# A deep cross network on one core: tail operand kept in two lane orders, 512-column row tiles, corner among the row tiles, new head and tail order

## The chip, the cores and the metric

The kernel runs on 1 core of one Trainium2 chip. The metric is the time of one execution on the device in microseconds (us). Before the change it is 141.67 us, the median of 3 runs.

Engines, by the names of the profile: PE is TensorE (matmuls; PEld are its weight loads), DVE is VectorE, ACT is ScalarE, POOL is GpSimd, SP is SyncE, which here only issues DMAs. PE reads SBUF and writes PSUM, here 8 banks of 512 fp32 columns on 128 partitions (the tensor `ps`); DVE and ACT read it from there.

## The reference

```python
B, F, D, L = 4096, 26, 16, 6
Din = min(F * D, 1024)

def reference(x0, ws, bs):
    x = x0
    for l in range(ws.shape[0]):
        x = x0 * (x @ ws[l] + bs[l]) + x
    return x
```

`x0` is 4096 x 416, `ws` six matrices of 416 x 416, `bs` six rows of 416, all bf16. Since x is x0 times some factor at every layer, x = x0 * s, the kernel keeps the sum of all `x @ ws[l]` so far in PSUM and never clears it between layers: after layer l, x = x0 * (1 + sums + biases up to l). That is one DVE instruction per tile, (PSUM + bias) * x0, where the bias column holds 1 plus the sum of the biases.

## The kernel before

**Tiles.** The 4096 rows of x are worked in four stages (`s`) of 1024. Everything is held transposed: features on partitions, rows of x on columns. The 416 features are three chunks of 128 (`m` for outputs, `k` for inputs) and a tail of 32. Each of the three chunks has two halves of 512 rows (`half`), which fill PSUM banks 0 to 2 and 3 to 5. The tail's 1024 rows are folded: group `g` of 256 rows lies on the partitions 32g to 32g + 31 (a lane) of one tile with 256 columns, in bank 6. Bank 7 (`SPARE`) is for transposes.

**One layer on PE** (the loop over `l` in L212 to L299), in program order:

1. `main(0)`: for each of three output chunks and three input chunks four matmuls of 32 output columns each, which lie side by side in the array (column tiles, `tile_mm`), each 128 x 32 weights against 512 columns: 36 matmuls, half 0.
2. Row tiles (L264 to L280): the tail as input, 32 partitions deep, for all three chunks and both halves: 12 matmuls of 256 columns. Lane g sits in the row group 32g of the array. The tail group g belongs to half g // 2 and to columns (g % 2) * 256 of that half's banks, so lanes 0 and 1 write into the same banks, and lanes 2 and 3. [...]
3. The tail as output: 12 column tiles of 256 columns from the three chunks, and 4 more with the corner of the matrix (tail to tail) from `wc_sb`, a block-diagonal copy of the corner that POOL makes with eight copies (`corner`, L144).
4. `main(1)`: half 1, 36 column tiles.

**Around it.** DVE takes each of the six banks of a layer with one instruction of 128 x 512 (L348) and writes `xT_sb` (or `xo_sb` in the last layer). It waits for `s_ti` (row tiles done) for half 0 and for `s_mb` for each chunk of half 1. PE's next `main(0)` waits for half 0 (`s_xa`), its next row tiles for half 1 (`s_xb`) and for the tail (`s_xt`). The tail goes from bank 6 by ACT (L387, adds the bias) to `t32_sb`, and POOL (L158) multiplies it by x0's tail (`x0t_sb`) into `xt_sb`. x0's tail is brought in by small PE transposes (`tail_transposes`) and an ACT copy (`tail_in`), for stage 0 between `main(0)` and the row tiles of the first layer, for the others in layers 1 to 3 of stage 0.

**Start.** SP issues the two halves of `xin_sb` (the first 512 rows), a piece of the tail, a DMA transpose of rows 512 to 1023 and then weights; ACT issues the weights of layer 0, the biases and the tail's weights of layer 0. PE runs 20 dummy matmuls of 128 columns (`NFILL`) and then transposes `xin_sb` chunk by chunk as the two halves land; DVE and ACT copy the results to `x0T_sb`.

**End.** The first three stages leave by DMA transposes. The last stage is transposed by PE (L312) after DVE's last instructions, ACT and DVE copy the results to `o_sb`, and SP issues four stores of 208 KB.

Of the kernel before, what the change touches and what calls it, by code (L numbers as in the profile page):

```python
# [11 lines left out]
def bass_standalone__dcn_v2_cross__recsys_kernel(  # L12
# [8 lines left out]
    NC = 3  # L21
# [9 lines left out]
    TAIL, SPARE = 6, 7  # L31
    NFILL = 20

    with ExitStack() as es:
# [6 lines left out]
        wt_sb = sb("wt_sb", [128, L, D])  # L41
        wc_sb = sb("wc_sb", [128, L, 128])
# [3 lines left out]
        x0t_sb = sb("x0t_sb", [128, NS, G])  # L46
        xT_sb = sb("xT_sb", [128, 2, NC, SB])
        xt_sb = sb("xt_sb", [128, 2, G])
        t32_sb = sb("t32_sb", [128, 2, G], FP32)
        xo_sb = sb("xo_sb", [128, NS, NC, SB])  # L50
# [4 lines left out]
        ones_sb = sb("ones_sb", [128, 128])  # L55
# [17 lines left out]
        s_tp, s_te = sem("s_tp"), sem("s_te")  # L73
        s_row, s_ti, s_to, s_mb = sem("s_row"), sem("s_ti"), sem("s_to"), sem("s_mb")
        s_xa, s_xb = sem("s_xa"), sem("s_xb")
        s_ta, s_xt = sem("s_ta"), sem("s_xt")
        s_oT, s_ot, s_otc = sem("s_oT"), sem("s_ot"), sem("s_otc")
        s_pT, s_out = sem("s_pT"), sem("s_out")
        s_oet, s_oe = sem("s_oet"), [sem("s_oe%d" % i) for i in range(4)]
# [6 lines left out]

        @block.sync
        def _(sp):
            for h in range(2):
                sp.dma_start(xin_sb[:, 2 * h:2 * h + 2, :], x0_v[:, 2 * h:2 * h + 2, :]).then_inc(s_xin[h], 16)  # L90
            sp.dma_start(xtl_sb[:, 4:JS, :], x0_v[:, 4:JS, DF:D]).then_inc(s_xtl0, 16)
            sp.dma_start_transpose(x0T_sb[:, :, H:SB], x0[H:SB, 0:DF]).then_inc(s_x0T[0], 16)
            for l in range(1, L):
                sp.dma_start(w_sb[:, l, :, :], wmain(l)).then_inc(s_w[l], 16)
                if l == 1:
                    for g in range(4):
                        sp.dma_start(
                            wt_sb[32 * g:32 * g + 32, 1:L, :], ws[1:L, DF:D, :].rearrange("l p n -> p l n")
                        ).then_inc(s_wt[1], 16)
# [20 lines left out]
            for i in range(4):  # L120
                j = (NS - 1) * JS + 2 * i
                if i == 0:
                    sp.wait_ge(s_oet, 1)
                sp.wait_ge(s_oe[i], 1)
                sp.dma_start(out_v[:, j:j + 2, :], o_sb[:, j:j + 2, :]).then_inc(s_out, 16)
            sp.wait_ge(s_out, 16 * (NS + 3))

        @block.gpsimd
        def _(pool):
            pool.memset(ones_sb[:, :], 1.0).then_inc(s_ones, 1)  # L130
            pool.memset(bsa_sb[0:1, :], 1.0).then_inc(s_set, 1)
            pool.wait_ge(s_ones, 1)
            pool.affine_select(
                out=ident[:, :], in_=ones_sb[:, :], pattern=[[-1, 128]],
                compare_op=ALU.is_equal, fill=0.0, base=0, channel_multiplier=1,
            ).then_inc(s_set, 1)
            pool.affine_select(
# [4 lines left out]
            pool.wait_ge(s_set, 4)  # L142

            def corner(i, a, b):  # L144
                pool.wait_ge(s_wt[i], 64)
                for g in range(4):
                    p = slice(32 * g, 32 * g + 32)
                    pool.tensor_copy(out=wc_sb[p, a:b, p], in_=wt_sb[p, a:b, DF:D]).then_inc(s_wc, 1)  # L148
                    pool.wait_ge(s_wc, 4 * i + g + 1)

            corner(0, 0, 1)
            for s in range(NS):
                pool.wait_ge(s_te, s + 1)
                for l in range(L):
                    n = s * L + l + 1
                    pool.wait_ge(s_ta, n)
                    dst = xot_sb[:, s, :] if l == L - 1 else xt_sb[:, (l + 1) % 2, :]
                    pool.tensor_tensor(  # L158
                        out=dst, in0=t32_sb[:, n % 2, :], in1=x0t_sb[:, s, :], op=ALU.mult
                    ).then_inc(s_xt, 1)  # L160
                    if n == 1:
                        pool.wait_ge(s_xt, 1)
                        corner(1, 1, L)
# [8 lines left out]
        def _(pe):  # L172
            def tile_mm(dst, lhsT, rhs, q, start, stop):
                return pe.matmul(  # L174
                    dst, lhsT=lhsT, rhs=rhs, start=start, stop=stop,
                    skip_group_check=True, tile_position=(0, 32 * q),
                )

            def tail_transposes(s):
                for r in range(2):  # L180
                    for g in range(4):
                        j = 2 * g + r
                        src = xin_sb[:, j, DF:D] if s == 0 and j < 4 else xtl_sb[:, s * JS + j, :]
                        ins = tile_mm(
                            ps[32 * g:32 * g + 32, SPARE, r * 128:(r + 1) * 128],
                            src, ident[:, :], g, True, True,
                        )
                ins.then_inc(s_tp, 1)

            pe.wait_ge(s_ones, 1)  # L190
            for i in range(NFILL):
                pe.matmul(ps[:, SPARE, 0:128], lhsT=ones_sb[:, :], rhs=ones_sb[:, :], start=True, stop=True)  # L192
            pe.wait_ge(s_set, 4)
            for h in range(2):
                pe.wait_ge(s_xin[h], 16)
                for c in range(NC):
                    for j in range(2 * h, 2 * h + 2):
                        ins = pe.transpose(  # L198
                            out=psT[:, NC * (1 - h) + c, (j % 2) * 128:(j % 2 + 1) * 128],
                            in_=xin_sb[:, j, c * 128:(c + 1) * 128], identity=ident[:, :],  # L200
                        )
                    ins.then_inc(s_inT, 1)
            pe.wait_ge(s_bs, 16)
            for c in range(NC):
                for q in range(4):
                    f0 = c * 128 + 32 * q
                    ins = tile_mm(ps[32 * q:32 * q + 32, SPARE, c * 8:c * 8 + L], bsa_sb[:, f0:f0 + 32], u_sb[:, :], q, True, True)
            for q in range(4):
                ins = tile_mm(ps[32 * q:32 * q + 32, SPARE, NC * 8:NC * 8 + L], bsa_sb[:, DF:D], u_sb[:, :], q, True, True)
            ins.then_inc(s_cbp, 1)  # L210

            for s in range(NS):  # L212
                for l in range(L):
                    n = s * L + l
                    if l == 0:
# [6 lines left out]
                    def main(half, waits):  # L222
                        o = off + half * H
                        for m in range(NC):
                            for k in range(NC):
                                if waits and m == 0:
                                    waits(k)
                                for q in range(4):
                                    f0 = m * 128 + 32 * q
                                    ins = tile_mm(  # L230
                                        ps[32 * q:32 * q + 32, NC * half + m, :],
                                        w_sb[:, l, k, f0:f0 + 32], src[:, k, o:o + H], q,
                                        l == 0 and k == 0 and half == 0, True,
                                    )
                            if half == 1:
                                ins.then_inc(s_mb, 1)

                    def wait_a(k):
                        if n > 0:
                            pe.wait_ge(s_xa, NC * (n - 1) + k + 1)  # L240
                        if n == 0:
                            pe.wait_ge((s_inD, s_inA, s_inD)[k], (3, 2, 4)[k])
                        elif l == 0 and k == 0:
                            pe.wait_ge(s_x0T[s], 16)
# [3 lines left out]
                    main(0, wait_a)  # L248

                    if n == 0:  # L250
                        pe.wait_ge(s_xtl0, 16)
                        pe.wait_ge(s_cb, 1)
                        tail_transposes(0)
                    if s == 0 and l < 2:
                        pe.wait_ge(s_wt[l], 64)
                        pe.wait_ge(s_wc, 4 * (l + 1))
                    if n == 0:
                        pe.wait_ge(s_te, 1)
                    else:
                        pe.wait_ge(s_xt, n)  # L260
                        pe.wait_ge(s_xb, NC * n)
# [173 lines left out]
```

## Time and profile before

| | |
|---|---|
| median of 3 runs | 141.67 us (141.16, 141.67, 142.47) |
| the profiled execution's own time | 141.47 us |
| its span, first to last instruction | 138.9 us |
| granted TensorE clock, mean | 0.989 |
| PE busy | 131.3 us, 2506 matmuls |
| DVE busy | 98.7 us, 149 instructions |
| ACT, POOL busy | 17.7 us, 21.1 us |
| HBM read, written | 3.22 MB, 3.41 MB |

The times of single instructions and waits are from the profiled execution. A line such as `57.20 0.76 PE L272 MATMUL ps<-xt_sb,wt_sb 32*128 32x256 bf16 x12` of the timeline means: from 57.20 us after the start of the span, for 0.76 us, twelve matmuls of line 272, weights 32 deep and 128 wide, against 256 columns. Such a matmul's duration holds its way through the array; the next may begin long before it ends, so the pace is read from starts. What stands in brackets is the idle time of the engine before the line, and what ended it. In the chain of work a line is a start, a length and what it was.

### The profile page before, as it was taken

The numbers are of one execution on the slowest core, as the hardware profiler recorded it, in microseconds if no ns is written. First come the engines' busy times: TensorE is split into PE (matmuls) and PEld (weight loads), VectorE is DVE, ScalarE is ACT, GpSimd is POOL, SyncE is SP. The second block draws the span as 40 slices with busy tenths as digits, with TensorE's granted clock in tenths as the row PEclk, the third lists the DMA queues.
The fourth block names the chain that finished last, engine by engine and source line by source line (L and its number), as shares of the span: only waits on it lengthen the run. The fifth ranks groups of instructions, "written<-read, shape, count | busy, mean of one in ns | idle before, by whom it ended". The sixth has DMA issues, their size and how long they took to land.

```text
span 138.9 us, 5386 instructions
## 1 busy us (share of the span) xinstructions
PE 131.3 (94%) x2506; PEld 67.2 (48%) x2506; DVE 98.7 (71%) x149; ACT 17.7 (13%) x36; POOL 21.1 (15%) x44
## 2 busy tenths in 40 slices
PE   6799999999999999999999999999999999999950
PEld 5435445545445545545445445545545445444440
DVE  0306797696697697688688679679669669669660
ACT  0601011121001001101101101101101101101170
POOL 5022211011011021011011021101101201101100
PEclk9999999999999999999999999999999999999995
DMA  4999799910008933000009652000009960000007
GB/s 118 267 245 329 99 218 233 195 33 0 5 0 76 176 126 129 0 5 0 5 0 118 133 168 82 5 0 5 5 0 186 65 221 29 5 0 7 0 1 244
DMA packets 32946, 12.26 MB, mean 88 GB/s; under 512 B 25239, under 2 KB 32925, under 8 KB 32925
## 3 DMA queue, kind: packets, MB, share of 16 engines
q1 hardware_dynamic: 32320, 11.50, 41.3%
q10 hardware_dynamic: 604, 0.43, 1.1%
q8 instruction: 19, 0.31, 1.0%
q14 instruction: 3, 0.02, 0.0%
HBM read 3.22 MB, written 3.41 MB: 48 GB/s over the span
## 4 chain that ended last, share of the span: by engine, by line
PE 90%; DVE 3%; DMA 3%; ACT 1%; SPq 0%; issue 0%
PE ps L174 77%; PE ps L272 12%; DVE xo_sb L348 3%; DMA xin_sb<-in_x_dram 3%; PE ps L312 1%; PE ps L198 1%; ACT o_sb L403 1%; SPq L90 0%; ACT x0t_sb L377 0%
## 5 line engine op out<-in xcount | busy, mean ns | idle before, releaser
L348 DVE SCALAR_TENSOR_TENSOR xT_sb<-ps,cb_sb,x0T_sb 128x512 bf16<-128x512 f32 x120 | 80.9, 743 | 26.1 <-PE ps L272 26.1
L174 PE MATMUL ps<-xT_sb,w_sb 128*32 128x512 bf16 (+1 forms) x1680 | 91.1, 364 | 0.0
L174 PEld LDWEIGHTS ps<-xT_sb,w_sb 128*32 128x32 bf16 x1680 | 42.9, 97 | 37.2
L158 POOL TENSOR_TENSOR xt_sb<-t_sb,x0t_sb 128x256 bf16<-128x256 f32 x20 | 13.5, 674 | 86.3 <-ACT t_sb L387 86.3
L387 ACT ACTIVATE t_sb<-ps,cb_sb 128x256 f32<-128x256 f32 x24 | 11.4, 474 | 103.0 <-PE ps L174 103.0
L174 PE MATMUL ps<-x0T_sb,w_sb 128*32 128x512 bf16 (+1 forms) x336 | 20.4, 389 | 0.0
L348 DVE SCALAR_TENSOR_TENSOR xo_sb<-ps,cb_sb,x0T_sb 128x512 bf16<-128x512 f32 x24 | 16.2, 744 | 4.3 <-PE ps L272 4.3
L272 PE MATMUL ps<-xt_sb,wt_sb 32*128 32x256 bf16 x240 | 15.2, 274 | 0.0
L174 PEld LDWEIGHTS ps<-x0T_sb,w_sb 128*32 128x32 bf16 x336 | 9.0, 101 | 8.4 <-issue 1.6
L272 PEld LDWEIGHTS ps<-xt_sb,wt_sb 32*128 32x128 bf16 x240 | 6.0, 91 | 13.5 <-issue 8.5
L174 PE MATMUL ps<-xt_sb,wc_sb 128*32 128x256 bf16 x80 | 5.7, 273 | 0.0
L158 POOL TENSOR_TENSOR xot_sb<-t_sb,x0t_sb 128x256 bf16<-128x256 f32 x4 | 2.7, 674 | 17.8 <-ACT t_sb L387 17.8
L330 DVE COPY x0T_sb<-ps 128x256 bf16<-128x256 bf16 x4 | 1.2, 292 | 5.2 <-PE ps L198 5.0
L272 PE MATMUL ps<-x0t_sb,wt_sb 32*128 32x256 bf16 x48 | 3.0, 274 | 0.6 <-ACT x0t_sb L377 0.6
L192 PE MATMUL ps<-ones_sb 128*128 128x128 bf16 x20 | 2.3, 313 | 1.1 <-POOL ones_sb L130 1.1
L148 POOL COPY wc_sb<-wt_sb 32x32 bf16<-32x32 bf16 (+1 forms) x8 | 2.1, 258 | 5.7 <-DMA wt_sb<-in_ws_dram 5.3
L272 PEld LDWEIGHTS ps<-x0t_sb,wt_sb 32*128 32x128 bf16 x48 | 1.2, 91 | 3.0 <-issue 2.0
L198 PE MATMUL ps<-ident,xin_sb 128*128 128x128 bf16 x12 | 1.6, 305 | 1.1 <-DMA xin_sb<-in_x_dram 1.1
L377 ACT ACTIVATE x0t_sb<-ps 128x256 bf16<-128x256 f32 x4 | 1.5, 383 | 8.4 <-PE ps L174 8.4
L403 ACT ACTIVATE o_sb<-ps 128x768 bf16<-128x768 bf16 x3 | 2.3, 809 | 2.2 <-PE ps L312 2.2
L192 PEld LDWEIGHTS ps<-ones_sb 128*128 128x128 bf16 x20 | 2.0, 147 | 1.1 <-POOL ones_sb L130 1.1
L312 PE MATMUL ps<-ident,xo_sb 128*128 128x128 bf16 x24 | 1.7, 220 | 0.8 <-DVE xo_sb L348 0.8
(28 smaller groups left out, 16.2 us busy)
## 6 DMA issues: line engine op xcount, KB each, us to landing
out_dram<-o_sb SPq DMA_DIRECT2D x3, 832.0 KB, 4.2
w_sb<-in_ws_dram SPq DMA_DIRECT2D x5, 312.0 KB, 4.9
out_dram<-o_sb SPq DMA_DIRECT2D x4, 208.0 KB, 2.4
wt_sb<-in_ws_dram SPq DMA_DIRECT2D x4, 130.0 KB, 3.9
xin_sb<-in_x_dram SPq DMA_DIRECT2D x2, 208.0 KB, 3.5
w_sb<-in_ws_dram ACTq DMA_DIRECT2D x1, 312.0 KB, 3.8
xtl_sb<-in_x_dram SPq DMA_DIRECT2D x1, 192.0 KB, 7.3
o_sb<-xo_sb SPq DMA_TRANSPOSE x9, 4.4
```

The source lines that it names most:

```text
L148: pool.tensor_copy(out=wc_sb[p, a:b, p], in_=wt_sb[p, a:b, DF:D]).then_inc(s_wc, 1)
L158: pool.tensor_tensor(out=dst, in0=t32_sb[:, n % 2, :], in1=x0t_sb[:, s, :], op=ALU.mult).then_inc(s_xt, 1)
L174: return pe.matmul(dst, lhsT=lhsT, rhs=rhs, start=start, stop=stop, skip_group_check=True, tile_position=(0, 32 * q),)
L192: pe.matmul(ps[:, SPARE, 0:128], lhsT=ones_sb[:, :], rhs=ones_sb[:, :], start=True, stop=True)
L198: ins = pe.transpose(out=psT[:, NC * (1 - h) + c, (j % 2) * 128:(j % 2 + 1) * 128], in_=xin_sb[:, j, c * 128:(c + 1) * 128], identity=iden ...
L272: ins = pe.matmul(ps[:, NC * (g // 2) + m, (g % 2) * G:(g % 2) * G + G], lhsT=wt_sb[p, l, m * 128:(m + 1) * 128], rhs=srct[p, :], start=l ...
L312: ins = pe.transpose(out=psT[:, banks[i], jj * DF + c * 128:jj * DF + (c + 1) * 128], in_=xo_sb[:, s, c, j * 128:(j + 1) * 128], identity= ...
L330: dve.tensor_copy(out=x0T_sb[:, c, h * 256:(h + 1) * 256], in_=psT[:, NC * (1 - h) + c, 0:256]).then_inc(s_inD, 1)
L348: dve.scalar_tensor_tensor(out=dst, in0=ps[:, NC * half + c, :], scalar=cb_sb[:, c, l:l + 1], in1=x0T_sb[:, c, o:o + H], op0=ALU.add, op1= ...
L377: act.activation(out=x0t_sb[:, s, :], in_=ps[:, SPARE, 0:G], func=ACTF.Copy).then_inc(s_te, 1)
L387: act.activation(out=t32_sb[:, n % 2, :], in_=ps[:, TAIL, 0:G], func=ACTF.Identity, bias=cb_sb[:, NC, l:l + 1],).then_inc(s_ta, 1)
L403: act.activation(out=o_sb[:, j0 + 2 * i:j0 + 2 * i + 2, 0:DF], in_=psT[:, (SPARE, 0, 3, 4)[i], 0:2 * DF].rearrange("p (j d) -> p j d", d=D ...
```

## The change

The change has five parts.

**The tail in two lane orders.** `xt_sb` and `x0t_sb` become twice as wide. The left half is what it was; in the right half lanes 0 and 1 have changed places, and lanes 2 and 3. ACT makes the right half with four copies of 32 partitions (`swap_lanes`) after POOL's product; for x0's tail of stage 0 PE makes a second set of transposes and DVE copies it, for the later stages ACT does it in layer 2. In lanes 0 and 2 the two halves together are 512 columns: the whole of a half of a stage, in order.

**Row tiles.** A row tile of lane 0 (or 2) is now 512 columns and fills a whole bank. In `part` 0 lane 0 does bank 0 and lane 1 bank 2, as two matmuls of 256 columns; lanes 2 and 3 do the same with banks 3 and 5. In `part` 1 lane 0 does bank 1 and lane 2 bank 4; lanes 1 and 3 do the corner, into banks 6 and 7. So no two lanes share a bank at any time, and `s_row` and its waits are gone. `wt_sb` holds, per lane, only the columns that the lane needs, and `wc_sb` (with 32 zero columns more) is filled by two POOL DMAs; the eight copies are gone.

**The tail as output** lies in two banks (6 for lanes 0 and 1, 7 for 2 and 3), and ACT evicts it in two halves of 64 partitions. Its four column tiles for the corner are gone. The spare halves of banks 6 and 7 take the transposes of x0's tail, one stage per stage, in layer 1.

```diff
-                    for i, jobs in enumerate((
-                        ((0, 0), (1, 1), (2, 0), (3, 1)), ((0, 2), (2, 2)),
-                        ((0, 1), (1, 0), (2, 1), (3, 0)), ((1, 2), (3, 2)),
-                    )):
-                        if i >= 2:
-                            pe.wait_ge(s_row, 3 * n + i - 1)
-                        for g, m in jobs:
...
+                    def row(g, dst, lhsT, cols, start):
+                        return pe.matmul(
+                            dst, lhsT=lhsT, rhs=srct[lane(g), cols], start=l == 0 and start, stop=True,
+                            skip_group_check=True, tile_position=(32 * g, 0),
+                        )
+
+                    lo, hi = slice(0, G), slice(G, 2 * G)
+                    for part in range(2):
+                        for h in range(2):
+                            g, wm = 2 * h, slice(part * 128, part * 128 + 128)
+                            row(g, ps[:, NC * h + part, :], wt_sb[lane(g), l, wm], slice(0, H), h == 1)
+                            g += 1
+                            if part == 0:
+                                row(g, ps[:, NC * h + 2, hi], wt_sb[lane(g), l, 0:128], lo, h == 1)
+                            else:
+                                row(g, ps[:, 6 + h, lo], wc_sb[lane(g), l, 0:128], lo, True)
+                        for h in range(2):
+                            g = 2 * h + 1
+                            if part == 0:
+                                ins = row(g, ps[:, NC * h + 2, lo], wt_sb[lane(g), l, 0:128], hi, False)
+                            else:
+                                ins = row(g, ps[:, 6 + h, lo], wc_sb[lane(g), l, 32:160], hi, False)
                     ins.then_inc(s_ti, 1)
...
+            def swap_lanes(buf, done):
+                for g in range(4):
+                    ins = act.activation(out=buf[lane(g), G:2 * G], in_=buf[lane(g ^ 1), 0:G], func=ACTF.Copy)
+                ins.then_inc(done, 1)
...
+                    if l < L - 1:
+                        act.wait_ge(s_xt, n)
+                        swap_lanes(xt_sb[:, (l + 1) % 2, :], s_sw)
```

PE's order in a layer, before. In these rows `xT_sb` and `w_sb` are the chunks and their weights, `xt_sb`, `wt_sb` and `wc_sb` the tail, its weights and its corner; 32x512 is a column tile, 128x256 a row tile.

```order
L174 MATMUL ps<-xT_sb,w_sb 32x512 x36
L272 MATMUL ps<-xt_sb,wt_sb 128x256 x12
L174 MATMUL ps<-xT_sb,w_sb 32x256 x12
L174 MATMUL ps<-xt_sb,wc_sb 32x256 x4
L174 MATMUL ps<-xT_sb,w_sb 32x512 x36
```

PE's order in a layer, after.

```order
L312 MATMUL ps<-xt_sb,wt_sb 128x512
L312 MATMUL ps<-xt_sb,wt_sb 128x256
L312 MATMUL ps<-xt_sb,wt_sb 128x512
L312 MATMUL ps<-xt_sb,wt_sb 128x256 x3
L312 MATMUL ps<-xt_sb,wt_sb 128x512
L312 MATMUL ps<-xt_sb,wc_sb 128x256
L312 MATMUL ps<-xt_sb,wt_sb 128x512
L312 MATMUL ps<-xt_sb,wc_sb 128x256 x3
L195 MATMUL ps<-xT_sb,w_sb 32x256 x12
L195 MATMUL ps<-xT_sb,w_sb 32x512 x72
```

The corner stands among the row tiles, and the tail's column tiles are followed by the chunks at once. ACT's order after, from the first layer of stage 0 on; before, each layer had the single eviction `t_sb` of 128x256, and the copies to `x0t_sb` in layers 1 to 3.

```order
L468 ACTIVATE t_sb<-ps,cb_sb 64x256 x2
L450 ACTIVATE xt_sb<-xt_sb 32x256 x4
L468 ACTIVATE t_sb<-ps,cb_sb 64x256 x2
L476 ACTIVATE x0t_sb<-ps 64x256 x2
L450 ACTIVATE xt_sb<-xt_sb 32x256 x4
L468 ACTIVATE t_sb<-ps,cb_sb 64x256 x2
L450 ACTIVATE xt_sb<-xt_sb 32x256 x4
L450 ACTIVATE x0t_sb<-x0t_sb 32x256 x4
```

A layer has six ACT instructions where it had one, and four of them stand between POOL's product and PE's next row tiles.

**Head.** The dummy matmuls are 13 of 256 columns, and 3 more between the two halves of the transposes. The second half of `xin_sb` is issued by ACT, layer 0's weights by SP behind the first half; the tail's weights of layer 0 are split between SP and ACT. In the first layer the tail's transposes, now 16, stand between chunks 1 and 2 of half 0.

```diff
-                pe.matmul(ps[:, SPARE, 0:128], lhsT=ones_sb[:, :], rhs=ones_sb[:, :], start=True, stop=True)
+            fill(13)
...
+                fill((3, 0)[h])
...
-            for h in range(2):
-                sp.dma_start(xin_sb[:, 2 * h:2 * h + 2, :], x0_v[:, 2 * h:2 * h + 2, :]).then_inc(s_xin[h], 16)
+            sp.dma_start(xin_sb[:, 0:2, :], x0_v[:, 0:2, :]).then_inc(s_xin[0], 16)
+            sp.dma_start(w_sb[:, 0, :, :], wmain(0)).then_inc(s_w[0], 16)
...
+            act.dma_start(xin_sb[:, 2:4, :], x0_v[:, 2:4, :]).then_inc(s_xin[1], 16)
...
+                    chunk(0, 0, before_a)
+                    chunk(1, 0)
                     if n == 0:
                         pe.wait_ge(s_xtl0, 16)
+                        tail_transposes(0)
+                    chunk(2, 0)
```

**End.** In the last layer chunk 2 of half 0 is evicted by ACT into `a32_sb` (fp32) and multiplied by POOL; DVE has five tiles in place of six. The first half's output is transposed by narrow column tiles (`out_tile`, 32 x 128, fp32 results) before and after the last chunk of half 1. ACT copies the first half and the tail to `o_sb`, DVE the second half. Three stores replace four: SP issues 4 and 2 row blocks, ACT the last 2.

```diff
+                        if n == NL - 1 and half == 0 and c == 2:
+                            continue
...
+                    chunk(0, 1).then_inc(s_mb, 1)
+                    chunk(1, 1).then_inc(s_mb, 1)
+                    if last:
+                        pe.wait_ge(s_xa, NC * NL - 1)
+                        pe.wait_ge(s_a32, 1)
+                        pe.wait_ge(s_ta, NL)
+                        for i in range(2):
+                            for j in range(2 * i, 2 * i + 2):
+                                for c in range(2):
+                                    ins = out_tile(c, j, A_OUT[j], c * 128)
+                            ins.then_inc(s_pA, 1)
+                    chunk(2, 1).then_inc(s_mb, 1)
...
+            sp.wait_ge(s_oet, 1)
+            sp.wait_ge(s_oeA, 3)
+            sp.dma_start(out_v[:, j:j + 4, :], o_sb[:, j:j + 4, :]).then_inc(s_out, 16)
+            sp.wait_ge(s_oeD, 2)
+            sp.dma_start(out_v[:, j + 4:j + 6, :], o_sb[:, j + 4:j + 6, :]).then_inc(s_out, 16)
...
+            act.wait_ge(s_oet, 1)
+            act.wait_ge(s_oeD, 2)
+            act.dma_start(out_v[:, j0 + 6:j0 + 8, :], o_sb[:, j0 + 6:j0 + 8, :]).then_inc(s_out, 16)
```

339 lines of the change are left out of this document (184 added, 155 removed).

## The prediction

> **What bounds the kernel now.** I read the page's busy shares and its chain of work first, then the chain in order of time for the length of a layer, then the timeline of one layer in the middle, and last the timelines of the start and the end. The first two lines are the page's busy times and granted clock, the third the chain by engine, the others the chain in order of time (start, length, what): the first and last of 24 layers, and two neighbours in the middle.
>
> ```profile
> PE 131.3 (94%) x2506; PEld 67.2 (48%) x2506; DVE 98.7 (71%) x149; ACT 17.7 (13%) x36; POOL 21.1 (15%) x44
> PEclk9999999999999999999999999999999999999995
> ...
> PE 90%; DVE 3%; DMA 3%; ACT 1%; SPq 0%; issue 0%
> ...
> 10.71 0.76 PE ps L272 x12
> ...
> 57.27 0.69 PE ps L272 x12
> 57.97 4.43 PE ps L174 x88
> 62.40 0.69 PE ps L272 x12
> ...
> 129.07 0.71 PE ps L272 x12
> ```
>
> TensorE carries the chain from 6 to 130 us, and a layer is 62.40 - 57.27 = 5.13 us: 0.69 of row tiles (L272) and 4.43 of column tiles (L174). The timeline of that layer tells where the 0.69 goes.
>
> ```profile
> 56.88 0.39 PE L174 MATMUL ps<-xT_sb,w_sb 128*32 128x512 bf16 x4
> 57.20 0.76 PE L272 MATMUL ps<-xt_sb,wt_sb 32*128 32x256 bf16 x12
> 57.32 0.53 PE L272 MATMUL ps<-xt_sb,wt_sb 32*128 32x256 bf16 x6
> 57.56 0.19 PEld L272 LDWEIGHTS ps<-xt_sb,wt_sb 32*128 32x128 bf16 x6 [0.25 <-PE ps L272]
> 57.69 0.28 PE L272 MATMUL ps<-xt_sb,wt_sb 32*128 32x256 bf16 x2
> 57.90 0.51 PE L174 MATMUL ps<-xT_sb,w_sb 128*32 128x256 bf16 x12
> 58.01 4.04 DVE L348 SCALAR_TENSOR_TENSOR xT_sb<-ps,cb_sb,x0T_sb 128x512 bf16<-128x512 f32 x6 [1.08 <-PE ps L272]
> 58.23 0.28 PE L174 MATMUL ps<-xt_sb,wc_sb 128*32 128x256 bf16 x4
> 58.34 0.60 PE L174 MATMUL ps<-xT_sb,w_sb 128*32 128x512 bf16 x8
> 58.57 0.47 ACT L387 ACTIVATE t_sb<-ps,cb_sb 128x256 f32<-128x256 f32 x1 [4.65 <-PE ps L174]
> 59.12 0.67 POOL L158 TENSOR_TENSOR xt_sb<-t_sb,x0t_sb 128x256 bf16<-128x256 f32 x1 [4.45 <-ACT t_sb L387]
> ```
>
> Four matmuls that lie side by side in the array I call a group. The two 512-column groups from 58.34 last 0.60, and one alone (from 56.88) 0.39, so groups of 512 columns follow each other by 0.21 us (0.216 at the ratio that the layer's sum asks for). The corner group follows the last tail group and takes 58.34 - 58.23 = 0.11. The row tiles come in four groups, at 57.20, 57.32, 57.57 and 57.69: steps of 0.12, 0.25 and 0.12. The step of 0.25 is the `s_row` wait: PEld sat 0.25 us until L272's own matmuls ended. On both sides the array turns between column and row tiles: 57.20 - 56.88 - 0.21 = 0.10 in, 57.90 - 57.69 - 0.11 = 0.10 out. DVE ends at 58.01 + 4.04 = 62.05 and the next row tiles start at 62.33: DVE is about 0.2 us from being the bound, ACT and POOL are far.
>
> **The steady layer.** The corner's group leaves: -0.11. The row tiles become, per row group of the array, 512 columns in `part` 0 and 512 in `part` 1, in rows 0 and 2 as one matmul, in rows 1 and 3 as two of 256. No wait stands between them, since each row group owns its banks. I take starts at 0, 0.12, 0.24, 0.36 (the 0.12 between two groups of 256 that share row groups, twice measured above), where before it was 0, 0.12, 0.37, 0.49: -0.13. Both turns stay at 0.10. A layer becomes 5.13 - 0.24 = 4.89. The step that was not seen is a 512 beside two 256 in other rows. At best the rows follow each other by their streaming of 0.11: -0.27. At worst in this mechanism each of the two steps inside rows 1 and 3 costs 0.05 more for weights: -0.14. I take -0.24, because the row nearest to it is the 0.12. Over 23 layers from the first row tiles to the last that is **-5.5 us** (-3.2 to -6.2). The eight transposes after the tail come in three layers before and in three now, and cancel.
>
> What could take the place of PE. DVE: it starts 58.01 - 57.69 = 0.32 after the last row group and takes 4.04; a TensorE instruction that waits for DVE starts 0.06 after it (133.84 to 133.90 in the end rows below). The loop is 0.36 + 0.32 + 4.04 + 0.06 = 4.78, under 4.89 by 0.11. So DVE does not bind, but its cover is nearly gone: anything that makes PE's layer shorter than 4.78 buys nothing.
>
> ACT gets new work on a path that TensorE waits for (`s_sw`): two halves of the tail's eviction, then POOL's product, then four copies between lanes. From the first row group: out of the row tiles at 0.36 + 0.21 = 0.57, three tail groups of 0.11, ACT starts 0.34 after the last of them is issued (58.57 - 58.23): 1.13. For the price of two in a row and of a copy I use these rows.
>
> ```profile
> 10.18 0.38 ACT L377 ACTIVATE x0t_sb<-ps 128x256 bf16<-128x256 f32 x1 [3.64 <-PE ps L174]
> 132.73 1.51 ACT L403 ACTIVATE o_sb<-ps 128x768 bf16<-128x768 bf16 x2 [1.90 <-PE ps L312]
> L403 ACT ACTIVATE o_sb<-ps 128x768 bf16<-128x768 bf16 x3 | 2.3, 809 | 2.2 <-PE ps L312 2.2
> ```
>
> Two of 0.81 took 1.51, so a second one costs 0.70, 0.11 less than alone. The halves: 0.47 + 0.36 = 0.83, to 1.96. POOL: 0.08 + 0.67, to 2.71. The four copies, which no row shows (32 partitions, SBUF to SBUF): 0.08 + 3 x 0.27 + 0.38 = 1.27 by the copy from PSUM, to 3.98, and 1.9 if each took 0.47 alone, to 4.7. TensorE asks for them at 4.89. Hidden at both ends. Behind the waiting copies stands only the next layer's eviction, due at 6.02; in layer 2 four more copies (x0's tail) end by 5.2. In layer 1 the two spare evictions fill the time in which ACT waits for POOL anyway.
>
> **The start.** The start's timeline, then the load of the first weights (KB, us to landing), and two DMA lines of the code, each with its time to landing.
>
> ```profile
> 1.06 2.31 PE L192 MATMUL ps<-ones_sb 128*128 128x128 bf16 x20 [1.06 <-POOL ones_sb L130]
> 4.12 0.80 PE L198 MATMUL ps<-ident,xin_sb 128*128 128x128 bf16 x6 [0.75 <-DMA xin_sb<-in_x_dram]
> 5.26 0.82 PE L198 MATMUL ps<-ident,xin_sb 128*128 128x128 bf16 x6 [0.33 <-DMA xin_sb<-in_x_dram]
> 6.21 3.81 PE L174 MATMUL ps<-x0T_sb,w_sb 128*32 128x512 bf16 x36
> 10.71 0.76 PE L272 MATMUL ps<-x0t_sb,wt_sb 32*128 32x256 bf16 x12 [0.59 <-ACT x0t_sb L377]
> 11.85 2.12 PE L174 MATMUL ps<-x0T_sb,w_sb 128*32 128x512 bf16 x36
> 1.80 0.73 POOL L141 MEMSET wc_sb<- 128x768 bf16 x1
> w_sb<-in_ws_dram ACTq DMA_DIRECT2D x1, 312.0 KB, 3.8
> L92 SPq DMA_TRANSPOSE x0T_sb<-in_x_dram x1: 2716/2716/2716, 2.3 to 2.3; - x1
> DMA to landing us min/median/max: 5.6/5.6/5.6
> L363 ACTq DMA_DIRECT2D wt_sb<-in_ws_dram x4: 317/443/486, 2.0 to 3.3; - x4
> DMA to landing us min/median/max: 3.5/3.9/4.4
> ```
>
> The same 36 matmuls take 3.81 us from 6.21 and 2.12 from 11.85: at the start TensorE runs at half pace (the row of granted clocks has its 9 there too; it does not tell of this). Before, PE sits idle between 3.4 and 4.12 and between 4.92 and 5.26, and the full pace comes only at the end of those 36 (3.81 is nearly nine groups of 0.43, the last from about 9.6). Now 13 dummies of 256 columns (0.21 each at half pace) run from 1.17 (the ones tile is twice as wide: +0.1) to 3.94, six transposes from 4.12 to 4.76, three dummies to 5.40, six transposes to 6.04, the biases to 6.25. One gap of 0.2 is left. If unbroken work brings the full pace, as it did here after 4.4 us of it (5.26 to 9.6), it is there before 6.25, and the 36 take 9 x 0.216 = 1.94. The tail's transposes are now 16 (0.2) and stand ahead of chunk 2, which hides ACT's and DVE's copies of them (0.38 each) and removes the 0.59 that TensorE waited for ACT. First row tiles at 6.25 + 1.94 + 0.2 + 0.1 = 8.5, against 10.71: -2.2. If the pace still changes at 9.66, six groups at 0.43, 0.43 of transposes and three groups of which two are fast give 10.2: -0.5.
>
> [...]
>
> DMAs moved: `xin`'s second half goes to ACT's queue (earlier), `w_sb` 0 behind `xin` on SP (issue 1.3 in place of 0.8, landing 3.8 later at 5.1, needed at 6.25), SP's transpose of x0 starts 1.0 later (3.3 in place of 2.32) and lands 5.6 after that, 8.9, needed at 8.5 + 0.57 = 9.1: just hidden. The corner blocks come by two POOL DMAs, which no row shows: issued at about 3 and 3.5 (the fill of `wc_sb` ended at 2.53 and is wider now), with the weights' 3.5 to 4.4 us they are there by 7.9; with the slowest landing of the start, 5.6, by 9.1, which would hold the first row tiles by 0.6. The four POOL copies and their waits leave. I take **-1.7 us** for the start (-0.5 to -2.6, where an early pace shortens the transposes too).
>
> **The end.** From the last row tiles (129.00) on:
>
> ```profile
> 129.00 0.76 PE L272 MATMUL ps<-xt_sb,wt_sb 32*128 32x256 bf16 x12
> 129.80 4.04 DVE L348 SCALAR_TENSOR_TENSOR xo_sb<-ps,cb_sb,x0T_sb 128x512 bf16<-128x512 f32 x6 [1.08 <-PE ps L272]
> 133.90 0.84 PE L312 MATMUL ps<-ident,xo_sb 128*128 128x128 bf16 x12 [0.76 <-DVE xo_sb L348]
> 134.55 1.97 SPq L125 DMA_DIRECT2D out_dram<-o_sb  x4
> L125 SPq DMA_DIRECT2D out_dram<-o_sb x4: 372/476/502, 134.5 to 136.0; - x4
> DMA to landing us min/median/max: 2.1/2.4/2.5
> ```
>
> The first of four stores is issued 5.55 after the last row tiles, the last lands at 136.0 + 2.5 = 138.5, 9.5 after them. Now ACT and POOL take one of the six DVE tiles, the first half's transposes stand among the last layer's chunks, and three stores replace four. ACT: tile 2 evicted by 0.68 + 0.69 = 1.37 (0.47 and 256 more columns), the tail halves by 2.2. TensorE: chunks 0 and 1 end at 2.2, 32 narrow transposes 0.44, chunk 2 0.65, 16 more 0.22: 3.6, then the tail's eight. ACT's last two copies follow (0.6 and 0.4) to 4.8, the first store goes at 4.9, and DVE (five tiles to 4.35, transposes, two copies) frees the other two at 5.6. If the four landings, 0.6 apart for 208 KB each, are limited by the transfer, the last lands 3.95 after the first issue, as before: 8.85, so **-0.65 us**. If only the last issue counts: 5.6 + 2.5 = 8.1, -1.4. If a wait of ACT or POOL eats the lead: 0. I take the first, because the even landings speak for a full transfer path.
>
> **The sum.** -5.5 - 1.7 - 0.65 = -7.85. The profiled execution took 141.47 us (span 138.9 and 2.6 around it): 133.6. It lies 0.2 under the median of 141.67; I leave that, since the moment of the full pace differs from run to run. All terms at their good ends give 141.47 - 6.2 - 2.6 - 1.4 = 131.3, at their bad ends 141.47 - 3.2 - 0.5 = 137.8.
>
> **Rivals.**
> A. A matmul of 256 columns behind one of 512 does not end before it. Then rows 1 and 3 hold their first half until 0.22, and the starts become 0, 0.22, 0.33, 0.55 in place of 0.36: a layer of 5.08, only 0.05 gained, 1.2 in all: 141.47 - 1.2 - 1.7 - 0.65 = 137.9. For it: before, all row tiles are equal, so no row shows otherwise. Against it: the pair at 57.32 started while nothing but its own row groups had come free. In a bad case of it (0.6 at the start, nothing at the end) the time is within 1%.
> [...]
> B. The full pace comes no earlier, because transposes or the gap at 4 us count against it: 141.47 - 5.5 - 0.5 - 0.65 = 134.8. For it: before, work with gaps from 1.06 to 6.21 did not bring it.
> C. The change doesn't do what it says: the third row group stays 0.25 behind the second because weights cannot go ahead of matmuls in their own row group. Only the corner is gained, 23 x 0.11 = 2.5: 136.6. Against it: PEld's weights for the second pair went ahead without a gap.
> D. Slower: the lane copies end after TensorE asks for them. It decides when a layer passes 5.13 + 2.35/23 = 5.23, the start and the end gaining 2.35: 2.71 + 0.08 + 4x + 0.06 = 5.23, x = 0.59 us a copy. With 0.70 each (the spacing of the 768-column copies) a layer is 5.65 and the time 141.47 + 23 x 0.52 - 2.35 = 151.1. Against it: 256 columns took 0.38 from PSUM.
>
> **How the numbers follow.** My forecast 0.60, A 0.13, B 0.14, C 0.05, D 0.08. The likeliest is 133.6. The range reaches from the good ends, 131.3, to A, 137.9, and takes in B and C; what lies outside is D and A's upper part. A measurement of this kernel can tell about 1% (1.4 us) from no change. Faster by over 1%: the forecast, B, C and 0.09 of A, 0.88; within 1%: 0.04 of A; slower: D, 0.08.
>
> **What would show it.** A layer of 4.89 in the chain, row tiles with starts at 0, 0.12, 0.24 and 0.36 and no PEld wait on L312; DVE idle of some 0.85 a layer; ACT's copies ended 0.8 before the next row tiles. First row tiles at 8.5 to 9, the first 36 column tiles in about 2.1. First store of the last stage 4.9 after the last row tiles. Wrong would be: TensorE idle before L312 released by ACT (D) or DVE, starts of 0.22 in rows 1 and 3 (A), 36 column tiles still in over 3 us (B).

## The result, and the profile after

| | before | changed |
|---|---|---|
| median | 141.41 us (4 runs, 141.12 to 142.47) | 135.28 us (4 runs, 134.21 to 136.91) |
| profiled execution, its span | 141.47 us, 138.9 us | 136.91 us, 135.2 us |
| ratio of the times, 95% interval | | 0.953 (0.943 to 0.963) |

The time forecast was 133.6 us with a range of 131.3 to 137.9. The time lies in it, 1.7 us above the forecast. The four executions of the changed kernel differ by 2.7 us, and the profiled one is the slowest of them.

The page of the changed kernel, busy times, TensorE's slices, the granted clock, and the chain by engine and by line:

```profile
PE 127.0 (94%) x2456; PEld 65.6 (49%) x2456; DVE 99.3 (73%) x150; ACT 68.0 (50%) x156; POOL 21.9 (16%) x39
...
PE   6999389999999999999999999999999999999970
...
PEclk9999959999999999999999999999999999999997
...
PE 84%; SPq 6%; DMA 6%; issue 1%; DVE 1%; DVEq 0%
PE ps L195 74%; PE ps L312 9%; DMA xtl_sb<-in_x_dram 6%; SPq L106 2%; SPq L119 2%; SPq L117 1%; DVE o_sb L423 1%; PE ps L374 0%; SPq L113 0%; SPq L112 0%; SPq L116 0%; DVEq L33 0%
```

Two marks of the row of slices are new: TensorE is idle for most of the fifth slice (the digit 3), and in the sixth its granted clock falls to half. The chain has a part that before had no place in it: 6% for the DMA into `xtl_sb`, x0's tail for stages 1 to 3, and SP's queue ahead of it. The chain in order of time (start, length, what) and the timeline at that place:

```profile
9.69 7.64 DMA xtl_sb<-in_x_dram
17.37 5.77 PE ps L195 x80
23.14 0.55 PE ps L312 x8
23.69 4.33 PE ps L195 x84
```

```profile
14.29 0.51 PE L195 MATMUL ps<-xT_sb,w_sb 128*32 128x256 bf16 x12
17.37 0.41 PE L195 MATMUL ps<-ident,xtl_sb 128*32 128x128 bf16 x8 [2.57 <-DMA xtl_sb<-in_x_dram]
17.56 5.58 PE L195 MATMUL ps<-xT_sb,w_sb 128*32 128x512 bf16 x72
23.07 0.60 PE L312 MATMUL ps<-xt_sb,wt_sb 32*128 32x512 bf16 x7
```

TensorE waits 2.57 us for that load in layer 1 of stage 0, and then takes 5.58 us for 72 column tiles that take 4.06 in experiment 1. The table by stretches (length, busy us of PE, PEld, DVE, ACT, POOL, then the granted clock) gives the reason for the second: the clock is granted at 0.52 behind the wait.

```profile
13.90:17.30 3.40, 0.90 (x24) 0.40 (x16) 2.07 (x3) 0.94 (x2) 0.67 (x1) 0.99 0.38 47
17.30:20.80 3.50, 3.43 (x40) 1.45 (x44) 1.16 (x2) 2.41 (x6) 0.00 (x0) 0.52 1.06 223
20.80:24.20 3.40, 3.40 (x76) 1.70 (x72) 1.54 (x3) 0.02 (x1) 0.00 (x0) 1.00 1.17 225
```

In the kernel before the same transposes stood behind the last chunk of the layer, and the load had landed by then. The issue's line and time to landing, and its reader:

```profile
L100 SPq DMA_DIRECT2D xtl_sb<-in_x_dram x1: 488/488/488, 9.7 to 9.7; - x1
...
DMA to landing us min/median/max: 7.3/7.3/7.3
```

```profile
18.92 0.28 PE L174 MATMUL ps<-ident,xtl_sb 128*32 128x128 bf16 x8
```

It landed at 9.7 + 7.3 = 17.0 and was read at 18.92. In the changed kernel it landed at 9.69 + 7.64 = 17.33, and TensorE asks for it from 14.8 on (14.29 + 0.51), because the transposes stand before the chunks of half 1 and the start is quicker.

A layer far from there, the changed kernel's timeline:

```profile
120.77 0.39 PE L195 MATMUL ps<-xT_sb,w_sb 128*32 128x512 bf16 x4
121.09 0.60 PE L312 MATMUL ps<-xt_sb,wt_sb 32*128 32x512 bf16 x7
121.32 0.27 PE L312 MATMUL ps<-xt_sb,wc_sb 32*128 32x256 bf16 x1
121.63 4.40 PE L195 MATMUL ps<-xT_sb,w_sb 128*32 128x256 bf16 x84
121.77 4.04 DVE L418 SCALAR_TENSOR_TENSOR xT_sb<-ps,cb_sb,x0T_sb 128x512 bf16<-128x512 f32 x6 [0.83 <-PE ps L312]
122.20 0.95 ACT L468 ACTIVATE t_sb<-ps,cb_sb 64x256 f32<-64x256 f32 x2 [1.44 <-PE ps L195]
123.23 0.68 POOL L182 TENSOR_TENSOR xt_sb<-t_sb,x0t_sb 128x256 bf16<-128x256 f32 x1 [4.20 <-ACT t_sb L468]
123.94 1.69 ACT L450 ACTIVATE xt_sb<-xt_sb 32x256 bf16<-32x256 bf16 x4 [0.79 <-POOL xt_sb L182]
125.96 0.60 PE L312 MATMUL ps<-xt_sb,wt_sb 32*128 32x512 bf16 x7
```

From row tiles to row tiles it is 125.96 - 121.09 = 4.87 us, against 5.13. The row tiles take 121.63 - 121.09 = 0.54, with the corner among them and without a gap; before it was 0.70, and 0.11 more for the corner. Part 1 starts 0.23 behind part 0.

### The profile page after: what moved, and what is told of

Read it like the earlier page. It is cut to its first block, busy times and chain, and to the rows that moved or that the text cites. A ratio compares the mean times of both kernels' runs of the same rounds, so it can differ in the third digit from the quotient of the medians.

```text
span 135.2 us, 5398 instructions
## 1 busy us (share of the span) xinstructions
PE 127.0 (94%) x2456; PEld 65.6 (49%) x2456; DVE 99.3 (73%) x150; ACT 68.0 (50%) x156; POOL 21.9 (16%) x39
## 3 DMA queue, kind: packets, MB, share of 16 engines
HBM read 2.90 MB, written 3.41 MB: 47 GB/s over the span
## 4 chain that ended last, share of the span: by engine, by line
PE 84%; SPq 6%; DMA 6%; issue 1%; DVE 1%; DVEq 0%
PE ps L195 74%; PE ps L312 9%; DMA xtl_sb<-in_x_dram 6%; SPq L106 2%; SPq L119 2%; SPq L117 1%; DVE o_sb L423 1%; PE ps L374 0%; SPq L113 0%; SPq L112 0%; SPq L116 0%; DVEq L33 0%
## 5 line engine op out<-in xcount | busy, mean ns | idle before, releaser
L468 ACT ACTIVATE t_sb<-ps,cb_sb 64x256 f32<-64x256 f32 x48 | 22.5, 469 | 38.3 <-PE ps L195 37.9
L450 ACT ACTIVATE xt_sb<-xt_sb 32x256 bf16<-32x256 bf16 x80 | 33.1, 414 | 14.4 <-POOL xt_sb L182 13.6
L312 PE MATMUL ps<-xt_sb,wt_sb 32*128 32x512 bf16 (+1 forms) x160 | 12.1, 326 | 0.1
L312 PE MATMUL ps<-xt_sb,wc_sb 32*128 32x256 bf16 x80 | 7.7, 268 | 0.0
L312 PEld LDWEIGHTS ps<-xt_sb,wt_sb 32*128 32x128 bf16 x160 | 2.5, 91 | 8.7 <-DVE xT_sb L418 8.3
L450 ACT ACTIVATE x0t_sb<-x0t_sb 32x256 bf16<-32x256 bf16 x12 | 5.0, 414 | 0.2
L202 PE MATMUL ps<-ones_sb 128*128 128x256 bf16 x16 | 3.8, 415 | 1.2 <-POOL ones_sb L153 1.2
L312 PEld LDWEIGHTS ps<-xt_sb,wc_sb 32*128 32x128 bf16 x80 | 4.0, 93 | 0.4
L476 ACT ACTIVATE x0t_sb<-ps 64x256 bf16<-64x256 f32 x6 | 2.3, 378 | 2.1 <-PE ps L195 2.0
L312 PE MATMUL ps<-x0t_sb,wt_sb 32*128 32x512 bf16 (+1 forms) x32 | 2.4, 326 | 0.0
```

Of the source, the lines that this page charges most:

```text
L202: pe.matmul(ps[:, 7, 0:256], lhsT=ones_sb[:, 0:128], rhs=ones_sb[:, :], start=True, stop=True)
L312: return pe.matmul(dst, lhsT=lhsT, rhs=srct[lane(g), cols], start=l == 0 and start, stop=True, skip_group_check=True, tile_position=(32 * ...
L450: ins = act.activation(out=buf[lane(g), G:2 * G], in_=buf[lane(g ^ 1), 0:G], func=ACTF.Copy)
L468: ins = act.activation(out=t32_sb[HALVES[h], n % 2, :], in_=tail(h), func=ACTF.Identity, bias=cb_sb[HALVES[h], NC, l:l + 1],)
L476: ins = act.activation(out=x0t_sb[HALVES[h], s + 1, 0:G], in_=spare(h), func=ACTF.Copy)
```

## Experiments

Experiments 1 and 2 start from the changed kernel, 3 to 7 from the kernel of experiment 1, since the late load would blur all smaller differences; 8 starts from experiment 7, 9 from the kernel before, and 10 joins several edits. They ran in three series on three chips (1 and 3 to 5; 6 to 9; 2 and 10), in which the kernel before had medians of 141.31, 141.19 and 140.98 us. So 0.3 us between two series tells little.

**1. The load earlier.** The DMA for `xtl_sb` is issued behind the weights of layer 1, ahead of those of layers 2 to 5.

```diff
                 if l == 1:
                     for g in range(4):
                         load_wt(sp, g, 1, L, s_wt[1])
+                    sp.dma_start(xtl_sb[:, JS:NJ, :], x0_v[:, JS:NJ, DF:D]).then_inc(s_xtl, 16)
-            sp.dma_start(xtl_sb[:, JS:NJ, :], x0_v[:, JS:NJ, DF:D]).then_inc(s_xtl, 16)
```

> The load of x0's tail for stages 1 to 3 (the DMA into xtl_sb) is issued ahead of the weights of layers 2 to 5, right behind those of layer 1; all else is the changed kernel. Theory (late load): TensorE stood idle from 14.75 to 17.37 us in the changed kernel because this load landed at 17.33, so the second row-tile interval (9.33 us) falls to that of its neighbours with transposes, 4.98, and the half pace that followed the idle time goes too: 136.91 - 4.35 = 132.6 against the profiled execution, and 2.6 under the quick executions of 134.2 to 134.6, so 131.5 to 132.6, all runs within 0.7. Rival (full path): the load is slow because the DMA engines are full between 3.5 and 28 us, so an earlier issue lands hardly earlier or pushes the weights of layer 2 past their need; 134.5 to 137 as before.

Measured: 132.44 us median of 6 (132.09 to 132.62), ratio to before 0.935 (0.931 to 0.939). Its load and its timeline at the same place:

```profile
L123 SPq DMA_DIRECT2D xtl_sb<-in_x_dram x1: 438/438/438, 7.9 to 7.9; - x1
...
DMA to landing us min/median/max: 5.2/5.2/5.2
```

```profile
14.51 0.28 PE L195 MATMUL ps<-ident,xtl_sb 128*32 128x128 bf16 x8
14.62 4.06 PE L195 MATMUL ps<-xT_sb,w_sb 128*32 128x512 bf16 x72
18.62 0.60 PE L312 MATMUL ps<-xt_sb,wt_sb 32*128 32x512 bf16 x7
```

The load lands at 7.9 + 5.2 = 13.1, the transposes start without a wait, the interval is 18.62 - 13.63 = 4.99, and the 72 column tiles take 4.06 again. The times now lie within 0.5 us. The theory held, and its rival, that an earlier issue lands hardly earlier, did not; the late load was worth 2.8 us of the median.

**2. The changed kernel once more,** unedited, in six executions.

> The changed kernel once more, unedited, beside e9_combined on the same chip. [...]

Measured: 134.26, 134.45, 134.52 and 136.21, 136.23, 136.33 us. The profiled one was of the first group (134.52):

```profile
16.47 0.30 PE L195 MATMUL ps<-ident,xtl_sb 128*32 128x128 bf16 x8 [2.16 <-DMA xtl_sb<-in_x_dram]
16.59 4.06 PE L195 MATMUL ps<-xT_sb,w_sb 128*32 128x512 bf16 x72
20.58 0.60 PE L312 MATMUL ps<-xt_sb,wt_sb 32*128 32x512 bf16 x7
```

```profile
17.30:20.80 3.50, 3.50 (x70) 1.65 (x66) 2.07 (x3) 1.95 (x5) 0.00 (x0) 1.00 1.06 231
```

Here TensorE waits 2.16 us, somewhat less than the 2.57 of the first profiled execution, and the clock is granted in full behind it (1.00); the interval is 20.58 - 13.25 = 7.33. So the wait is there in both profiled executions, and the half pace in one of them only. The two groups are 1.8 us apart, about what 3.4 us at half pace cost (1.7). The mean granted clock of every execution says the same: in both series of the changed kernel it is 0.994 or 0.995 in the five from 134.2 to 134.7 us, and 0.980 to 0.984 in the five from 135.9 to 136.9.

**3. A wait between the parts of the row tiles.**

```diff
...
                     for part in range(2):
+                        if part == 1:
+                            ins.then_inc(s_row, 1)
+                            pe.wait_ge(s_row, n + 1)
                         for h in range(2):
```

> Base is e1_tail_early. Part 1 of the row tiles now waits for the last matmul of part 0, as s_row made it wait in the kernel before. Theory (the wait was the cost that the whole banks removed): the start of part 1 moves from 0.23 to about 0.36 behind the first row tile, a layer from 4.875 to about 5.0, 24 layers +3.1 us on e1_tail_early. Rival (the third set was held by its weights or by the order of the matmuls, not by the wait): no change, under +0.5.

Measured: 138.37 us, +5.9 on experiment 1, with a layer of 5.14. TensorE and its weight loads there:

```profile
60.65 0.87 PE L313 MATMUL ps<-xt_sb,wt_sb 32*128 32x512 bf16 x7
61.14 0.28 PE L313 MATMUL ps<-xt_sb,wc_sb 32*128 32x256 bf16 x1
```

```profile
61.13 0.09 PEld L313 LDWEIGHTS ps<-xt_sb,wt_sb 32*128 32x128 bf16 x1 [0.37 <-PE ps L313]
```

Part 1 starts 0.49 behind part 0 in place of 0.23. The direction is the theory's, the price twice its own: 0.26 a layer, where I had taken 0.13 from the kernel before. In the kernel before the twelve row tiles come in four sets, and `s_row` lets the third wait for the first and the fourth for the second: there the wait was for the set before the last, and half of it lay beside the last set; here it is for the set just issued. So this wait is a harsher one than `s_row` was: it shows that a wait costs, not that the old one cost 0.13. It alone undoes the whole gain of a layer.

**4. The corner back to column tiles.** Part 1 keeps only rows 0 and 2; four column tiles follow the tail's twelve; POOL loads four blocks.

```diff
...
-                                row(g, ps[:, 6 + h, lo], wc_sb[lane(g), l, 0:128], lo, True)
...
-                                ins = row(g, ps[:, 6 + h, lo], wc_sb[lane(g), l, 32:160], hi, False)
...
+                    for g in range(4):
+                        ins = tile_mm(
+                            ps[lane(g), 6 + g // 2, 0:G], wc_sb[:, l, 32 * g:32 * g + 32], srct[:, 0:G], g, False,
+                        )
```

> Base is e1_tail_early. The corner goes back to four column tiles of 256 columns behind the tail's twelve; in part 1 only rows 0 and 2 work; POOL loads four corner blocks in place of two. Theory (the corner is free among the row tiles, since rows 0 and 2 stream 512 columns there anyway): one group of 0.11 more per layer, a layer of 4.98 in place of 4.875, +2.5 us over 23 layers, and up to +1 at the start, where two more POOL loads land before the first row tiles. Rival (rows 1 and 3 with their two halves set the end of the row tiles, so the corner costs there what it saves): +0.5 or less in the steady layers.

Measured: 134.63 us, +2.2, a little under the theory's 2.5. In the chain two layers start at 58.99 and 63.97, 4.98 apart:

```profile
58.99 0.54 PE ps L312 x6
59.53 4.44 PE ps L195 x88
63.97 0.54 PE ps L312 x6
```

The row tiles take 0.54 with or without the corner, the rest 4.44 in place of 4.33: the corner is free among the row tiles and costs 0.11 outside.

**5. No dummies at the start:** `fill(13)` becomes `fill(1)`.

> Base is e1_tail_early. One dummy matmul in place of 13 at the start; the three between the transposes stay. [...]

Measured: 133.32 us, +0.9. The first 24 column tiles in this kernel, then in experiment 1:

```profile
3.97 0.80 PE L229 MATMUL ps<-ident,xin_sb 128*128 128x128 bf16 x6 [2.40 <-DMA xin_sb<-in_x_dram]
...
6.17 2.67 PE L195 MATMUL ps<-x0T_sb,w_sb 128*32 128x512 bf16 x24
...
9.67 0.59 PE L312 MATMUL ps<-x0t_sb,wt_sb 32*128 32x512 bf16 x7
```

```profile
6.18 1.74 PE L195 MATMUL ps<-x0T_sb,w_sb 128*32 128x512 bf16 x24
```

Both start at the same time; without the dummies they last 0.93 longer, and the first row tiles come at 9.67 in place of 8.75.

**6. No dummies in the middle:** the three between the halves of the transposes are gone.

> Base is e1_tail_early (132.44). The three dummies between the two halves of the transposes are gone. Theory (they only cost time, since the second half of xin_sb landed at 3.93 and TensorE reaches it at 4.56): the first column tiles start 0.6 earlier, but the corner blocks land at 8.2 and the second half of x0 at 8.4, so the first row tiles gain 0.2 to 0.5 of it: 131.9 to 132.3. Rival (the dummies keep the work unbroken, without them the full pace comes later): 0.3 to 1 slower than e1_tail_early.

Measured: 132.13 us (132.01 to 132.32), 0.3 under experiment 1, about what a comparison across two series can tell. The trace is clearer: the column tiles start at 5.54 in place of 6.18, and then TensorE waits for the corner blocks, so that the first row tiles gain 0.25 (8.50 against 8.75).

```profile
5.54 1.48 PE L195 MATMUL ps<-x0T_sb,w_sb 128*32 128x512 bf16 x24
...
8.50 0.59 PE L311 MATMUL ps<-x0t_sb,wt_sb 32*128 32x512 bf16 x7 [0.61 <-DMA wc_sb<-in_ws_dram]
```

**7. x0's lane copies in the last layer of a stage** in place of layer 2 (`l == 2` becomes `l == L - 1` before `swap_lanes(x0t_sb...)`).

> Base is e1_tail_early. ACT's four copies of the next stage's x0 tail move from layer 2 of a stage to its last layer, where no copies of the tail itself stand. Theory (ACT's chain is what delays the row tiles by 0.10 once a stage, in the layer behind those copies): the three intervals of 4.975 become 4.875, -0.3 us: 132.1. Rival (DVE or a DMA makes those intervals longer): no change, or the first row tiles of the next stage come late by the 1.7 us of the copies less the slack of the last layer, up to +1.

Measured: 132.21 us (131.86 to 132.29). The interval behind those copies, 62.38 - 57.41 = 4.97 in the changed kernel, is 4.87 like its neighbours here, in all three stages that make these copies. The mechanism is shown in the trace; in the times the difference is 0.2 us, across two series, and that is less than they can tell.

**8. A fifth copy on ACT** in each layer, ahead of the four, into a tile that nobody reads; base is experiment 7.

```diff
...
+                        act.activation(
+                            out=pad_sb[0:32, :], in_=xt_sb[0:32, (l + 1) % 2, 0:G], func=ACTF.Copy
+                        )
                         swap_lanes(xt_sb[:, (l + 1) % 2, :], s_sw)
```

> Base is e6_swap_last. One more copy of 32 partitions x 256 in ACT's queue ahead of the four in each layer, into a tile that nobody reads. The prediction held ACT's chain to end 0.8 us before the row tiles that wait for it. By that, no change. Theory from the trace (a copy takes 0.42 and does not overlap the next, so the chain ends 0.3 before): the row tiles come 0.1 to 0.2 late in 20 layers, +2 to +4 us on e6_swap_last.

Measured: 136.65 us, +4.4 on experiment 7 and a little above the theory's 2 to 4, with a layer of 5.11. ACT and TensorE there:

```profile
61.77 0.42 ACT L481 ACTIVATE pad_sb<-xt_sb 32x256 bf16<-32x256 bf16 x1 [0.79 <-POOL xt_sb L183]
62.20 1.69 ACT L451 ACTIVATE xt_sb<-xt_sb 32x256 bf16<-32x256 bf16 x4
```

```profile
64.04 0.40 PE L313 MATMUL ps<-xt_sb,wt_sb 32*128 32x512 bf16 x6 [0.17 <-ACT xt_sb L451]
```

The copies end at 63.89 and the row tiles start 0.15 later, released by ACT. With the same 0.15 the chain of the changed kernel (1.69 from 123.94, then 0.15: 125.78) is 0.18 ahead of the row tiles at 125.96, and a copy of 0.42 more is 0.24 too late: 5.11 - 4.87. The prediction's 0.8 is refuted.

**9. The kernel before with its load earlier.**

> The kernel before, with its load of x0's tail for stages 1 to 3 moved ahead of the weights of layers 2 to 5 as in e1_tail_early. Theory (the load was late only against the new place of its reader; before, it landed at 17.05 and was read at 18.9): no change, within 0.4 us of the kernel before. Rival (issuing this load early helps or harms in any order, by the traffic of the start): a change of more than 0.5.

Measured: 141.36 us against 141.19 in the same series, ratio 1.000 (0.996 to 1.004). The load's place matters only with the changed order.

**10. Together:** experiments 1, 6 and 7, and the fill of `wc_sb` on DVE, so that POOL issues the corner blocks at 2.3 in place of 3.1.

> e1_tail_early with the moved x0 copies of e6_swap_last, without the three middle dummies (e5_no_middle), and with the fill of wc_sb on DVE in place of POOL, so that POOL issues the corner blocks about 1 us earlier. In e5_no_middle TensorE waited 0.61 for those blocks. Theory (start bound by the corner blocks): first row tiles at 7.9 to 8.1 in place of 8.5, and 0.3 less from the three intervals: 132.13 - 0.3 - 0.5 = 131.3. Rival (the second half of x0, landed at 8.44, binds right behind the first row tiles and eats the gain): 131.8 to 131.9.

Measured: 131.69 us median of 5 (131.37 to 131.91), ratio to before 0.934 (0.932 to 0.937). The first row tiles start at 7.98, as the theory had it; the time lies between the theory and its rival. This is the best version, 3.6 us under the changed kernel; some 2.8 of that is the load.

## Why the prediction was right or wrong

**The steady layer: right.** Forecast 4.89, measured 4.87. The starts of the parts, the 0.10 on both sides of the row tiles and the corner's 0.11 came as worked out. Experiment 4 shows the corner's half of it at its full size. Experiment 3 shows of the other half that a wait between the parts costs; the 0.13 itself is read from the starts (third set of row tiles at 0.37 before, second part at 0.23 now).

**Rival A fell in the trace.** The column tiles follow 0.54 behind the first row tile; with the starts of rival A it would have been 0.55 + 0.11 + 0.10 = 0.76. The trace has the second 256 of rows 1 and 3 start 0.12 behind the first. A 256 did not wait for the 512 ahead of it. The trace tells this by the starts alone; the ends are modelled there, so they tell nothing. (The bad case that the prediction puts within 1% is, by its terms, 141.47 - 1.2 - 0.6 = 139.7, or 1.3%.)

**Rivals C and D fell too.** Part 1 starts 0.23 behind part 0, without a wait of the weight loads (C), and TensorE does not wait for the lane copies but for 0.10 in three layers (D, and experiment 7). By the time alone, rival B's 134.8 is nearer to 135.28 than the forecast; only the traces tell them apart.

**The start: right in direction and size, but the moment of the full pace is not fixed.** Forecast -1.7, measured 8.87 against 10.71: -1.84. The sum had the full pace before 6.25. In this trace the groups of column tiles follow each other by 0.42 up to 7.00 and by 0.21 from there; in the kernel before the 0.42 lasts up to 9.59. The first 24 column tiles take 1.85 here, and in other profiled executions with these thirteen dummies 1.74 (experiment 1) and 1.48 (experiments 6 and 10); without the thirteen they take 2.67 (experiment 5). So the dummies bring the full pace earlier (rival B: no), and how much earlier is not the same in each. The one kernel differs too: its second row tiles come at 13.74 here and at 13.25 in experiment 2. The -1.7 itself was my estimate between the -2.2 and the -0.5 of the prediction's two cases; no run shows it as a term of its own, and in its place this trace has the -1.84. The three dummies in the middle cost time: the second half of `xin_sb` was there already (issued at 0.82, landed 3.1 later, where the three begin at 4.56). The corner's DMA landed before it was needed, but it is what binds once the rest is quicker (experiment 6).

**The end: right.** The first store is issued at 130.76, 4.80 behind the last row tiles (forecast 4.9), and the last lands at 131.62 + 3.2 = 134.8, 8.9 behind them (forecast 8.85). In the forecast's chain for TensorE, 2.2 + 0.44 + 0.65 + 0.22 adds up to 3.5 and not 3.6; nothing hangs on it.

```profile
130.76 0.37 SPq L146 DMA_DIRECT2D out_dram<-o_sb  x1
131.56 0.37 SPq L148 DMA_DIRECT2D out_dram<-o_sb  x1
131.62 0.43 ACTq L501 DMA_DIRECT2D out_dram<-o_sb  x1
...
out_dram<-o_sb ACTq DMA_DIRECT2D x1, 208.0 KB, 3.2
```

**What failed: the moved transposes.** The step read "the eight transposes after the tail come in three layers before and in three now, and cancel". Their durations cancel. Their wait does not: in layer 1 of stage 0 they read a load that lands at 17 us, and they moved from 18.9 to 14.8. I had the load's line in the code and in the list of DMAs moved spoke only of those whose issue moves. The wait costs 2.2 to 2.6 us in the profiled executions, and 1.8 more where the half pace follows: a term that the sum had at nothing. Experiments 1, 2 and 9 show it.

**What was mis-sized: ACT's copies.** I took 0.27 for each further copy, by two copies from PSUM that overlap; the four take 1.69, 0.42 each. The upper bound of 0.47 was the nearer end. It stayed hidden, but with 0.18 to spare in place of 0.8, and in three layers, each behind x0's own copies, it was late by 0.10, which the prediction did not have (experiments 7 and 8).

**What made up for it.** What lies around the span was 2.6 us in the profiled execution before and is 1.7 now. I had left it as it was. In the profiled executions of experiments 1 and 10 it is 1.8 (132.46 - 130.7 and 131.37 - 129.6). Over all executions beside the experiments it is 2.0 to 3.5 in the kernel before, and 1.7 to 1.9 in every changed version. Why it shrank and steadied is not settled; no run was aimed at it. The account of the profiled execution: 141.47 - 1.8 (start) - 5.6 (23 intervals, with 0.3 lost to ACT's copies already taken off) + 4.35 (the load, with the half pace) - 0.65 (end) - 0.9 (around the span) = 136.9. So the nearness of the time to the forecast is in part luck: without the late load the kernel takes 132.44 (experiment 1), 1.2 under the forecast, and the term that was missing and this one pull against each other.

## What to carry to other kernels

When a step is moved ahead, every operand that it reads gets an earlier due time, loads that the edit does not touch among them: set the landing of each against the new time of its reader. A wait on matmuls just issued cost 0.26 us a layer here, more than the 0.23 by which the parts otherwise follow each other, so giving each row group banks of its own was worth more than ordering the groups. After such a change look at how little each engine has left, in every layer and not only in a usual one: in the layer shown above DVE ends 0.15 before the next row tiles (121.77 + 4.04 = 125.81) and ACT's copies 0.33 (125.63), yet it was ACT that came late, in the three layers where x0's copies stood in its queue too.

## What the runs showed of the hardware

A TensorE idle time of 2.57 us was followed by half the clock for 3.41 us in one profiled execution, one of 2.16 us in another by none, and the times fall into two groups 1.8 us apart, with mean granted clocks of 0.980 to 0.984 and of 0.994 or 0.995. In the changed kernel's trace the granted clock is half from 17.23 and full again from 20.64:

```profile
17.23:20.64 3.41, 3.27 (x40) 1.39 (x44) 1.00 (x2) 2.41 (x6) 0.00 (x0) 0.50 1.08 230
20.64:24.05 3.41, 3.41 (x76) 1.72 (x72) 1.55 (x3) 0.00 (x0) 0.00 (x0) 1.00 1.16 221
```

The waits lie between 14.80 and 17.37 there and between 14.31 and 16.47 in experiment 2. They differ in length and in place, one profile stands on each side, and no run moved one without the other. So what decided between the half clock and the full one is not shown.

Four copies of 32 partitions x 256 from SBUF to SBUF on ACT took 1.69 us, 0.42 each, with no overlap to be seen. Two evictions of 64 partitions from PSUM took 0.95, 0.47 each, and did not overlap either; the two of 128 x 768 before the change did, by 0.11 (1.51 for two of 0.81).
